# Attention and two MLPs on one core: whole-chunk weight conversion, a shorter prologue, and other steps for the second MLP's weights

## Chip, core and metric

The kernel runs on one core of a Trainium2 chip. The metric is the device time of one execution in microseconds (us), as the median of three runs.

## What is computed

Sliding-window attention (four plain heads, four dilated) gives 2304 tokens of 512 features; two MLPs with 2048 hidden features follow. The weights come as float64, q, k and v as float32.

```python
scores = scale * np.matmul(q, k.transpose(0, 1, 3, 2))      # masked to a window
attn = softmax(scores); x = matmul(attn, v)                 # (2304, 512)
h = x @ w_in;  r = np.maximum(h, 0.0)
x = (s * (r * r) + b) @ w_out                               # first MLP
h = x @ w_in2; g = h * np.cos(h)
out = g @ w_out2                                            # second MLP
```

## The kernel before

Tokens are cut into five tiles (`SIZES` = 384, 384, 512, 512, 512), the hidden features into 16 chunks. A **step** `p` is one chunk of one tile of one MLP: steps 0 to 79 are the first MLP (tile = p // 16), 80 to 159 the second. In each step TensorE (PE) makes the hidden block h (`mm_in`), and two steps later adds the chunk to the four output blocks y (`mm_out`); ScalarE (ACT) and VectorE (DVE) make g from h in between (`relu2`). Tile 0 of the first MLP multiplies in full float32; all others split each operand into a high and a low part and use three passes.

Attention for tile 0 (8 units) runs ahead of all, as a **prologue** of steps k in the loop over `range(n0 + 4)`: scores and softmax of unit k, `a_norm` of k-1, `a_transpose` of k-3, `a_pv` of k-4. The other 40 units run in pairs, inside the MLP steps that `DUO` lists: scores (PE) and softmax (DVE, then ACT's exp) in step p, `a_norm` (DVE) and `a_transpose` (PE tp, then an ACT copy to pt) in p+1, `a_pv` (PE pv, reads pt) in p+2.

A float64 weight half-chunk (128x512; even k is w_in, odd k is w_out) is **converted** to float32: `w_load` (an SP DMA of 512 KB into a stage buffer, five of them), `w_float` (two ACT instructions, L117 and L118) and `w_join` (four DVE instructions, L124 to L133). For the first MLP `w_whole(n)` brings the joins up to half-chunk n, with one float ahead; `w_split` makes high and low parts in tiles 0 and 1. The second MLP's half-chunks are converted in the first MLP's tiles 1 to 4 (`BG` = 4, 8, 10 and 10 of them, evenly spread by a formula), cut into parts by `w_cut` one step later, written to DRAM, and fetched back by `w_fetch`.

Each engine runs its instructions in the order in which the program issues them; within a step that is `mm_in`, events of phase 0, the last `mm_out` of a tile, `w_point`, `relu2`, other `mm_out`s, events of phases 1 and 2.

Of the kernel before, what the change touches and what calls it, by code (L numbers as in the profile page):

```python
# [31 lines left out]
W_FIRST, W_STEPS = (7, 8, 9, 10), {8: 1, 9: 2, 11: 3}  # L32
# [4 lines left out]
WPRE, W_PACE = 4, 2.0  # L37
IN_CUT = 13

BG = (0, 4, 8, 10, 10)  # L40
PB, PK = 64, 96
# [13 lines left out]
def attention_then_two_mlps(ctx, tc, qk_p, qk_d, v_p, v_d, mask_p, mask_d, w1, w2, sv, bv, out):  # L55
# [7 lines left out]
    xspool = pool("xs", 4)  # L63
# [30 lines left out]
    last_two = []  # L94
    after_att = []

    def w_load(m, k, stage):  # L100
        raw_w[m, k] = stage
        nc.sync.dma_start(stage[:, :DM], (w1, w2)[m][k])

    def w_float(m, k):
        words = raw_w[m, k][:, :DM].bitcast(U32).rearrange("p (n two) -> p n two", two=2)
        low, high = words[:, :, 0], words[:, :, 1]
        if m == 0 and k + 2 < 2 * NFC:
            a = wpool.tile([P, DM], I32, tag=f"wl{k + 2}", name=f"wa{m}_{k}")
        elif m == 0:
            if not last_two:  # L110
                last_two.append(wpool.tile([P, 2, DM], I32, tag="raw2", name="last_two"))
            a = last_two[0][:, k % 2, :]
        else:
            a = late[0].tile([P, DM], I32, tag=f"wa{k % 2}", name=f"wa{m}_{k}")
        w32[m, k] = a
# [4 lines left out]
    def w_join(m, k):  # L120
        words = raw_w[m, k][:, :DM].bitcast(U32).rearrange("p (n two) -> p n two", two=2)
        low, high = words[:, :, 0], words[:, :, 1]
        a = w32[m, k]
# [11 lines left out]
    def w_split(k):  # L135
        a = w32.pop((0, k)).bitcast(F32)
        wh[0, k] = wpool.tile([P, DM], F32R, tag=f"wh{k}", name=f"wh0_{k}")
        wl[0, k] = wpool.tile([P, DM], F32R, tag=f"wl{k}", name=f"wl0_{k}")
        nc.scalar.copy(wh[0, k], a)
        nc.vector.tensor_tensor(out=wl[0, k], in0=a, in1=wh[0, k].bitcast(F32), op=ALU.subtract)  # L140


    def w_cut(k):
        a = w32.pop((1, k))
        hi = raw_w.pop((1, k)).bitcast(F32R)[:, :DM]
        cut[k] = scratch.tile([P, 2, DM], F32, tag=f"cut{k}", name=f"cut{k}")
        nc.scalar.copy(hi, a.bitcast(F32))
        nc.vector.tensor_tensor(out=a.bitcast(F32R), in0=a.bitcast(F32), in1=hi.bitcast(F32), op=ALU.subtract)
        nc.sync.dma_start(cut[k][:, 0, :], hi.bitcast(F32))
        nc.sync.dma_start(cut[k][:, 1, :], a.bitcast(F32))  # L150

    def w_fetch(k):
        wh[1, k] = wpool.tile([P, DM], F32R, tag=f"wh{k}", name=f"wh1_{k}")
        wl[1, k] = wpool.tile([P, DM], F32R, tag=f"wl{k}", name=f"wl1_{k}")
        nc.sync.dma_start(wh[1, k].bitcast(F32), cut[k][:, 0, :])
        nc.sync.dma_start(wl[1, k].bitcast(F32), cut[k][:, 1, :])
# [72 lines left out]
    def a_softmax(i):  # L229
# [3 lines left out]
        sm = d["place"](3, [nr, nb, nk]) if "place" in d else ap_.tile([nr, nb, nk], F32, tag="sm", name=f"sm{i}")  # L233
# [31 lines left out]
    def a_transpose(i, ps, copy=None):  # L265
        d = st[i]
        nb, nq, nk = d["nb"], d["nq"], d["nk"]
        nr = 2 * nq
        acc = ps.tile([P, 512], F32, tag=ps_tag[ps.name], name=f"tp{i}")
        for j in range(nb):  # L270
            nc.tensor.transpose(acc[:nk, j * nr : (j + 1) * nr], d["sm"][:, j, :], ident[:nr, :nr])  # L271
        pt = d["place"](4, [nk, 384]) if "place" in d else ap_.tile([nk, 384], F32, tag="pt", name=f"pt{i}")
        (copy or nc.vector.tensor_copy)(pt, acc[:nk, :384])
        d["pt"] = pt
# [37 lines left out]
    def x_split(m, t, cc):  # L312
        x = xspool.tile([P, 2, T], F32R, tag="xs", name=f"xs{m}_{t}_{cc}")[:, :, : SIZES[t]]
# [5 lines left out]
    def mm_in(m, t, fc, ps):  # L319
        h = ps.tile([P, 512], F32, tag=ps_tag[ps.name], name=f"h{m}_{t}_{fc}")  # L320
        hps[m, t, fc] = h
        for cc in range(NCC):
            cs = slice(cc * P, (cc + 1) * P)
            if m == 0 and t == 0:
                w = w32[m, 2 * fc].bitcast(F32)
# [5 lines left out]
            hi, lo = wh[m, 2 * fc][:, cs], wl[m, 2 * fc][:, cs]  # L331
# [4 lines left out]
    def mm_out(m, t, fc):  # L336
# [48 lines left out]
    whole_g = []  # L385

    def relu2(t, fc):
# [43 lines left out]
    with tc.manual_schedule():  # L431
# [4 lines left out]
        def w_load_to(n):  # L436
            while wq[0] < min(n, 2 * NFC):
                w_load(0, wq[0], stage.tile([P, DM], I64, tag=f"s{wq[0] % 5}", name=f"stage{wq[0]}"))
                wq[0] += 1

        def w_whole(n):

            q = wq
            n = min(n, 2 * NFC)
            while q[2] < n:
                while q[1] < min(q[2] + 2, 2 * NFC):
                    w_load_to(q[1] + 1)
                    w_float(0, q[1])
                    q[1] += 1
                w_join(0, q[2])  # L450
                q[2] += 1
            w_load_to(q[2] + 1 + AHEAD)

# [19 lines left out]
        for k in range(n0 + 4):  # L473
# [3 lines left out]
            if 0 <= k - 1 < n0:  # L477
                a_norm(k - 1)
            if 0 <= k - 3 < n0:
                a_transpose(k - 3, ps_a)  # L480
            if 0 <= k - 4 < n0:
                a_pv(k - 4, ps_y, f"y{k % NCC}")
            if k in W_STEPS:
                w_whole(W_STEPS[k])
# [29 lines left out]
        def w_point(p, half):  # L514
            if p < NFC:
                w_whole(int(W_PACE * (p + half / 2)) + WPRE)
            if half == 0 and 0 <= p - IN_CUT < NFC:
                w_split(2 * (p - IN_CUT))
            if half == 1 and 0 <= p - NFC < NFC:
                w_split(2 * (p - NFC) + 1)  # L520


        k = 0
        for t, n in enumerate(BG):
            for i in range(n):
# [3 lines left out]
                def load(k=k):  # L529
                    n = k % 2 if k < BG[1] else (k - BG[1]) % 3  # L530
                    place, tag = (late[0], f"raw{n}") if n < 2 else (wpool, "raw2")
                    w_load(1, k, place.tile([P, DM], I64, tag=tag, name=f"raw{k}"))

                at((p - 1, ph), load)
                at((p, ph), lambda k=k: w_float(1, k))
                at((p, ph), lambda k=k: w_join(1, k))
                at((p + 1, ph), lambda k=k: w_cut(k))
                k += 1
        assert k == 2 * NFC
# [5 lines left out]
        for p in range(NP + LAG[1]):  # L545
# [135 lines left out]
```

## Time and profile before

| | |
|---|---|
| median of three runs | 926.11 us (925.14 to 926.75) |
| the profiled execution | 924.52 us, its span 922.7 us |
| PE busy | 895.6 us (97%) |
| DVE busy | 590.2 us (64%) |
| ACT busy | 507.5 us (55%) |
| mean granted TensorE clock | 0.99 |

Times in the profile count from the first instruction. A PE row's end is modelled, so rows overlap; the distance between starts tells the real rate. Idle time in brackets stands with what ended it.

### The profile page before, as it was taken

Reading aid. Unit: us, or ns where it says so; the run is one execution under the profiler, and the core shown is the slowest. Engines: PE = TensorE matmul, PEld = TensorE weight load, DVE = VectorE, ACT = ScalarE, POOL = GpSimd, SP = SyncE. Lnnn points to the kernel's source line nnn. Section 1 sums busy time; section 2 is a strip of 40 time slices with the busy share of each in tenths; the row PEclk is TensorE's granted clock in tenths of the full one; section 3 lists DMA queues with packets and bytes.
Section 4 is the critical chain, followed back from the end, with each engine's and each line's share of the span. In section 5 each row is a group of like instructions: output and inputs, shape, how many; then the busy total and the mean of one; then the engine's idle time right before and its main releaser. Section 6 shows DMA issues by size and latency. Waiting matters only on the chain.

```text
span 922.7 us, 13285 instructions
## 1 busy us (share of the span) xinstructions
PE 895.6 (97%) x4888; PEld 755.4 (82%) x4888; DVE 590.2 (64%) x1160; ACT 507.5 (55%) x1162; POOL 0.7 (0%) x6
## 2 busy tenths in 40 slices
PE   6899999989999989999999999999999999999998
PEld 5566679889888877778888899999988888888886
DVE  6888868666565665557464766665755665566554
ACT  5767757666564654546353654645544554454443
POOL 0000000000000000000000000000000000000000
PEclk9799999999999999999999999999999999999999
DMA  9767424332534433436799700000000010001001
GB/s 261 245 224 241 138 72 156 105 119 88 173 129 138 143 122 125 156 101 215 251 319 309 256 16 1 20 16 1 20 15 1 1 45 1 1 1 47 0 1 46
DMA packets 45536, 99.64 MB, mean 108 GB/s; under 512 B 5440, under 2 KB 12064, under 8 KB 45472
## 3 DMA queue, kind: packets, MB, share of 16 engines
q1 hardware_dynamic: 45472, 98.80, 32.1%
q8 instruction: 39, 0.64, 0.3%
q14 instruction: 25, 0.20, 0.1%
HBM read 75.71 MB, written 23.07 MB: 107 GB/s over the span
## 4 chain that ended last, share of the span: by engine, by line
PE 88%; DVE 7%; ACT 3%; issue 1%; DMA 0%; SPq 0%; DVEq 0%
PE h L332 13%; PE h L333 13%; PE h L334 13%; PE y L349 12%; PE y L350 12%; PE y L351 12%; PE y L346 4%; PE h L326 4%; PE sc L220 2%; PE pv L283 2%; ACT sm L250 2%; PE tp L271 1%; DVE wa L133 1%; DVE wa L130 1%; DVE nmax L247 1%
## 5 line engine op out<-in xcount | busy, mean ns | idle before, releaser
L332 PE MATMUL h<-xs,wh 128*128 128x512 f32 (+1 forms) x576 | 218.6, 379 | 0.0
L349 PE MATMUL y<-g,wh 128*128 128x512 f32 (+1 forms) x576 | 214.9, 373 | 0.0
L333 PE MATMUL h<-xs,wh 128*128 128x512 f32 (+1 forms) x576 | 214.9, 373 | 0.0
L334 PE MATMUL h<-xs,wl 128*128 128x512 f32 (+1 forms) x576 | 214.8, 373 | 0.0
L351 PE MATMUL y<-g,wl 128*128 128x512 f32 (+1 forms) x576 | 213.7, 371 | 0.0
L350 PE MATMUL y<-g,wh 128*128 128x512 f32 (+1 forms) x576 | 213.6, 371 | 0.0
L332 PEld LDWEIGHTS h<-xs,wh 128*128 128x128 f32 x576 | 109.0, 189 | 15.7
L334 PEld LDWEIGHTS h<-xs,wl 128*128 128x128 f32 x576 | 108.8, 189 | 15.3
L333 PEld LDWEIGHTS h<-xs,wh 128*128 128x128 f32 x576 | 109.0, 189 | 14.8
L351 PEld LDWEIGHTS y<-g,wl 128*128 128x128 f32 x576 | 108.1, 188 | 15.1
L349 PEld LDWEIGHTS y<-g,wh 128*128 128x128 f32 x576 | 108.2, 188 | 14.8
L350 PEld LDWEIGHTS y<-g,wh 128*128 128x128 f32 x576 | 108.1, 188 | 14.7
L416 ACT ACTIVATE n<-n 128x512 f32<-128x512 f32 (+1 forms) x80 | 47.2, 590 | 102.5 <-DVE n L410 102.3
L406 ACT ACTIVATE n<-h,pmagic 128x512 f32<-128x512 f32 (+1 forms) x80 | 51.6, 646 | 87.0 <-PE h L334 86.9
L407 DVE TENSOR_SCALAR n<-n 128x512 f32<-128x512 f32 (+1 forms) x80 | 32.0, 400 | 86.6 <-ACT n L406 86.5
L422 DVE SCALAR_TENSOR_TENSOR n<-n,h 128x512 f32<-128x512 f32 (+1 forms) x80 | 50.7, 633 | 55.2 <-ACT n L417 55.2
L390 ACT ACTIVATE r<-h 128x512 f32<-128x512 f32 (+1 forms) x80 | 44.1, 551 | 67.3 <-PE h L334 58.8
L250 ACT ACTIVATE sm<-sm,nmax 96x80 f32<-96x80 f32 (+1 forms) x140 | 49.5, 355 | 46.1 <-DVE nmax L247 46.1
L400 DVE CAST g<-r 128x512 fp32r<-128x512 f32 (+1 forms) x64 | 26.1, 408 | 69.0 <-ACT r L398 59.5
L124 DVE TENSOR_SCALAR wa<-wa 128x512 f32<-128x512 f32 x62 | 26.2, 423 | 42.4 <-ACT wa L117 39.7
L410 DVE SCALAR_TENSOR_TENSOR n<-n,r 128x512 f32<-128x512 f32 (+1 forms) x80 | 51.1, 638 | 2.8
L409 DVE SCALAR_TENSOR_TENSOR r<-n,h 128x512 f32<-128x512 f32 (+1 forms) x80 | 50.7, 634 | 2.8
(81 smaller groups left out, 1060.6 us busy)
## 6 DMA issues: line engine op xcount, KB each, us to landing
stage<-w SPq DMA_DIRECT2D x32, 512.0 KB, 4.7
raw<-w SPq DMA_DIRECT2D x32, 512.0 KB, 4.6
cut<-raw SPq DMA_DIRECT2D x32, 256.0 KB, 2.1
cut<-wa SPq DMA_DIRECT2D x32, 256.0 KB, 2.5
wh<-cut SPq DMA_DIRECT2D x32, 256.0 KB, 3.9
wl<-cut SPq DMA_DIRECT2D x32, 256.0 KB, 4.4
qk<-qk_d SPq DMA_DIRECT2D x20, 352.0 KB, 3.4
qk<-qk_p SPq DMA_DIRECT2D x20, 304.0 KB, 2.9
```

Source lines behind the costliest of these rows:

```text
L250: nc.scalar.activation(out=sm[:, j, :], in_=sm[:, j, :], func=AF.Exp, bias=nmax[:, j : j + 1], scale=1.0, accum_out=ssum[:, j : j + 1],)
L332: nc.tensor.matmul(h[:, : SIZES[t]], hi, x[:, 0, :], start=cc == 0, stop=False)
L333: nc.tensor.matmul(h[:, : SIZES[t]], hi, x[:, 1, :], start=False, stop=False)
L334: nc.tensor.matmul(h[:, : SIZES[t]], lo, x[:, 0, :], start=False, stop=cc == NCC - 1)
L349: nc.tensor.matmul(y[:, : SIZES[t]], hi, g[:, 0, :], start=fc == 0, stop=False)
L350: nc.tensor.matmul(y[:, : SIZES[t]], hi, g[:, 1, :], start=False, stop=False)
L351: nc.tensor.matmul(y[:, : SIZES[t]], lo, g[:, 0, :], start=False, stop=fc == NFC - 1)
L406: nc.scalar.activation(out=n, in_=h[:, : SIZES[t]], func=AF.Identity, scale=1.0 / TWO_PI, bias=pmagic)
L409: nc.vector.scalar_tensor_tensor(out=r, in0=n, scalar=-C1, in1=h[:, : SIZES[t]], op0=ALU.mult, op1=ALU.add)
L410: nc.vector.scalar_tensor_tensor(out=n, in0=n, scalar=-C2, in1=r, op0=ALU.mult, op1=ALU.add)
L416: nc.scalar.activation(out=r, in_=r, func=AF.Sin, scale=0.5)
L422: nc.vector.scalar_tensor_tensor(out=r, in0=r, scalar=-1.0, in1=h[:, : SIZES[t]], op0=ALU.add, op1=ALU.mult)
```

## The change

Three things change.

1. **First MLP's weights.** Conversion goes by whole chunks (128x1024, both halves in one instruction) from chunk 4 on; chunks 0 to 3 go by halves, in the order of `W_ORDER` (chunk, first half, halves). `W_PACE` says how far the joins go in which step. Stage buffers are four whole chunks (two of them in the pool that later holds xs), chosen by chunk % 4. The split into parts is by whole chunks, in steps 14 to 29.
2. **Prologue.** One step shorter: transposes of k-2, pv of k-3; joins come after all its attention work.
3. **Second MLP's weights.** `BG_STEPS` lists the steps of each tile, none of which starts a pair of units; the cut comes at the start of the next step. The fetch is by whole chunks, both parts at once.

```diff
-W_FIRST, W_STEPS = (7, 8, 9, 10), {8: 1, 9: 2, 11: 3}
+W_FIRST, W_STEPS = (7, 8, 9, 10), {9: 1, 10: 3}
 DUO = ((), (3, 6, 9, 12), (0, 2, 5, 7, 10, 12), (0, 2, 5, 7, 10, 12), (1, 4, 8, 11))
-WPRE, W_PACE = 4, 2.0
-IN_CUT = 13
+W_ORDER = [(0, 0, 1), (1, 0, 1), (2, 0, 1), (0, 1, 1), (3, 0, 1), (1, 1, 1), (4, 0, 2), (2, 1, 1), (5, 0, 2), (3, 1, 1)]
+W_ORDER += [(f, 0, 2) for f in range(6, NFC)]
+W_PACE = [5, 6, 8, 9, 11] + [p + 7 for p in range(5, NFC)]
+CUT = 14
 BG = (0, 4, 8, 10, 10)
+BG_STEPS = ((), (3, 6, 9, 14), (1, 3, 4, 6, 8, 9, 13, 15), (0, 2, 3, 5, 6, 7, 9, 10, 13, 15), (0, 2, 3, 5, 6, 8, 10, 11, 13, 14))
...
+    def w1_load(fc, h, n):
+        if fc not in raw_w:
+            place, tag = ((stage, f"s{fc % 4}") if fc % 4 < 2 else (xspool, f"xs{fc % 2}"))
+            raw_w[fc] = place.tile([P, 2, DM], I64, tag=tag, name=f"stage{fc}")
+        for k in range(h, h + n):
+            nc.sync.dma_start(raw_w[fc][:, k, :], w1[2 * fc + k])
...
-        def w_whole(n):
+        def w_whole(n, more=1):
             q = wq
-            n = min(n, 2 * NFC)
-            while q[2] < n:
-                while q[1] < min(q[2] + 2, 2 * NFC):
+            n = min(n, len(W_ORDER))
+            while q[2] < n or q[1] < min(n + more, len(W_ORDER)):
+                while q[1] < min(q[2] + 1 + more, n + more, len(W_ORDER)):
                     w_load_to(q[1] + 1)
-                    w_float(0, q[1])
+                    w1_float(*W_ORDER[q[1]])
                     q[1] += 1
-                w_join(0, q[2])
-                q[2] += 1
-            w_load_to(q[2] + 1 + AHEAD)
+                if q[2] < n:
+                    w1_join(*W_ORDER[q[2]])
+                    q[2] += 1
+            w_load_to(q[2] + 1 + (AHEAD if q[2] < 10 else 2))
...
-        for k in range(n0 + 4):
+        for k in range(n0 + 3):
...
-            if 0 <= k - 3 < n0:
-                a_transpose(k - 3, ps_a)
-            if 0 <= k - 4 < n0:
-                a_pv(k - 4, ps_y, f"y{k % NCC}")
+            if 0 <= k - 2 < n0:
+                a_transpose(k - 2, ps_a)
+            if 0 <= k - 3 < n0:
+                a_pv(k - 3, ps_y, f"y{k % NCC}")
...
-                b = t * NFC + (2 if t == 1 else 0) + (i + 0.5) * (NFC - (2 if t == 1 else 0)) / n
-                p, ph = int(b), 1 + int(b % 1 >= 0.5)
...
+        for k, p in enumerate(t * NFC + step for t, steps in enumerate(BG_STEPS) for step in steps):
+            at((p - 1, 1), lambda k=k: w2_load(k))
+            at((p, 1), lambda k=k: w2_float(k))
+            at((p, 1), lambda k=k: w2_join(k))
+            at((p + 1, 0), lambda k=k: w2_cut(k))
```

**Order on ACT, step 4 of tile 0** (wa and stage: the weights of the half-chunk or chunk named; r and g: relu and its square; sm8, sm9: exp of the first pair; pt: copy of its transposes). Before:

```order
L250 ACTIVATE sm9_611,ssum9_615<-sm9_611,nmax9_613 128x96 x3
L117 ACTIVATE wa0_12_632<-stage12_559 128x512
L118 ACTIVATE stage12_559<-stage12_559 128x512
L390 ACTIVATE r0_4_641<-h0_0_4_619 128x384
L396 ACTIVATE g1_513<-r0_4_641 128x384
L117 ACTIVATE wa0_13_648<-stage13_585 128x512
L118 ACTIVATE stage13_585<-stage13_585 128x512
L273 COPY pt8_661<-tp8_657 96x384
L273 COPY pt9_667<-tp9_663 96x384
```

The same place in the change:

```order
L277 ACTIVATE sm9_566,ssum9_570<-sm9_566,nmax9_568 128x96 x3
L109 ACTIVATE wa6_587<-stage6_508 128x1024
L110 ACTIVATE stage6_508<-stage6_508 128x1024
L109 ACTIVATE wa7_594<-stage7_511 128x1024
L110 ACTIVATE stage7_511<-stage7_511 128x1024
L421 ACTIVATE r0_4_604<-h0_0_4_574 128x384
L425 ACTIVATE g1_109<-r0_4_604 128x384
L300 COPY pt8_615<-tp8_611 96x384
L300 COPY pt9_621<-tp9_617 96x384
```

Two whole chunks, 6 and 7, now stand between the exps and the copies of the first pair's transposes.

**Order on the SP queue, loads of tile 0** in the change (x2: both halves of a chunk):

```order
L135 DMA stage4_446<-w1 128x512 x2
L135 DMA stage2_160<-w1 128x512
L135 DMA stage5_468<-w1 128x512 x2
L135 DMA stage3_417<-w1 128x512
L135 DMA stage6_508<-w1 128x512 x2
L135 DMA stage7_511<-w1 128x512 x2
L231 DMA qk10_538<-qk_p 128x608
```

stage4 takes stage0's place and stage7 takes stage3's, so each load now waits for the last join that reads the chunk four before; in the old order a load waited for the half-chunk five before.

**Order on DVE, step 7 of tile 1** (sm22, sm23: a pair that starts there). Before:

```order
L247 TENSOR_REDUCE nmax23_1771<-sm23_1769 96x4
L124 TENSOR_SCALAR wa1_1_1778<-wa1_1_1778 128x512
L127 TENSOR_SCALAR wa1_1_1778<-wa1_1_1778 128x512
L130 SCALAR_TENSOR_TENSOR wa1_1_1778<-raw1_1693,wa1_1_1778 128x512
L133 ISA wa1_1_1778<-raw1_1693,wa1_1_1778 128x1024
L261 TENSOR_SCALAR ssum22_1764<-ssum22_1764 96x4
```

The same pair in the change:

```order
L123 ISA wa2_1_1534<-raw1_1489,wa2_1_1534 128x1024
L175 TENSOR_TENSOR wa2_1_1534<-wa2_1_1534,raw1_1489 128x512
L150 TENSOR_TENSOR wl0_9_1585<-wa9_683,wh0_9_1584 128x1024
L429 CAST g0_1_7_1591<-r1_7_1588 128x384
L430 TENSOR_TENSOR g0_1_7_1591<-r1_7_1588,g0_1_7_1591 128x384
L265 SCALAR_TENSOR_TENSOR sm22_1606<-sc22_1566,m_d_98 96x320
L274 TENSOR_REDUCE nmax22_1608<-sm22_1606 96x4
```

The join stood between the pair's maxima and its sums; now it and its cut stand ahead of the pair's first instruction.

## Rows read from the trace of the kernel before

**Rows 1.** The page: busy time of each engine, share of the span, instructions

```profile
PE 895.6 (97%) x4888; PEld 755.4 (82%) x4888; DVE 590.2 (64%) x1160; ACT 507.5 (55%) x1162; POOL 0.7 (0%) x6
```

**Rows 2.** Waits of PE over the span: total us, times, longest

```profile
PE tp L271 <- DVE ssum L261: 8.2, 4, 2.8
...
PE tp L271 <- DVE sm L263: 2.0, 7, 0.4
```

**Rows 3.** PE's timeline from 172.2 us: start, us, instruction, idle before

```profile
172.19 0.33 PE L350 MATMUL y<-g,wh 128*128 128x384 f32 x1
172.37 0.34 PE L351 MATMUL y<-g,wl 128*128 128x384 f32 x1
174.47 0.50 PE L271 MATMUL tp<-ident,sm 96*80 96x96 f32 x4 [1.77 <-DVE ssum L261]
```

**Rows 4.** Stretches, PE alone: stretch, PE busy (x), PEclk, DMA share, GB/s

```profile
194.80:198.10 3.30, 3.30 (x13) 0.50 0.24 88
...
345.00:348.30 3.30, 3.13 (x11) 0.50 0.10 37
```

**Rows 5.** DVE's timeline, tile 1, step 7

```profile
168.03 0.48 DVE L247 TENSOR_REDUCE nmax<-sm 96x4 f32<-96x320 f32 x1
171.08 0.43 DVE L124 TENSOR_SCALAR wa<-wa 128x512 f32<-128x512 f32 x1 [2.57 <-ACT wa L117]
...
173.44 0.16 DVE L261 TENSOR_SCALAR ssum<-ssum 96x4 f32<-96x4 f32 x1
```

**Rows 6.** ACT's timeline there, the instruction behind the last exp

```profile
170.41 0.64 ACT L117 ACTIVATE wa<-raw 128x512 f32<-128x512 f32 x1
```

**Rows 7.** DVE's timeline, tile 3, step 1

```profile
343.01 0.69 DVE L148 TENSOR_TENSOR wa<-wa,raw 128x512 fp32r<-128x512 f32 x1 [1.98 <-ACT raw L147]
```

**Rows 8.** DVE's timeline, end of the prologue and first steps of tile 0

```profile
22.92 0.55 DVE L273 COPY first<-tp 80x384 f32<-80x384 f32 x1
...
31.92 0.42 DVE L124 TENSOR_SCALAR wa<-wa 128x512 f32<-128x512 f32 x1
...
34.28 0.42 DVE L124 TENSOR_SCALAR wa<-wa 128x512 f32<-128x512 f32 x1
...
51.18 0.45 DVE L238 SCALAR_TENSOR_TENSOR sm<-sc,m_p 128x288 f32<-128x288 f32 x1
...
55.23 0.42 DVE L124 TENSOR_SCALAR wa<-wa 128x512 f32<-128x512 f32 x1
```

**Rows 9.** PE's timeline, tile 0: chunks 0 to 2, then 5 and 6

```profile
30.78 9.72 PE L326 MATMUL h<-xy,wa 128*128 128x384 f32 x24
...
55.80 2.75 PE L326 MATMUL h<-xy,wa 128*128 128x384 f32 x8
...
61.91 2.85 PE L326 MATMUL h<-xy,wa 128*128 128x384 f32 x8
```

**Rows 10.** Groups of DVE by form: busy us, mean ns, idle before

```profile
L401 DVE TENSOR_TENSOR g<-r,g 128x512 fp32r<-128x512 f32 x48 | 33.2, 693 | 1.6
...
L400 DVE CAST g<-r 128x512 fp32r<-128x512 f32 x48 | 20.4, 425 | 53.8 <-ACT r L398 44.2 <-PE sc L220 9.5
...
L401 DVE TENSOR_TENSOR g<-r,g 128x384 fp32r<-128x384 f32 x16 | 8.9, 559 | 0.6
L400 DVE CAST g<-r 128x384 fp32r<-128x384 f32 x16 | 5.7, 359 | 15.2 <-ACT r L398 15.2
```

**Rows 11.** DMA issues, 34 to 46 us: size, median us to landing

```profile
stage<-w SPq DMA_DIRECT2D x5, 512.0 KB, 3.3
```

**Rows 12.** DMA issues, 411 to 413 us (two loads 0.5 us apart)

```profile
raw<-w SPq DMA_DIRECT2D x2, 512.0 KB, 4.7
```

**Rows 13.** The loads of L102 between 30 and 70 us

```profile
DMA to landing us min/median/max: 3.1/4.3/6.8
```

**Rows 14.** ACT's timeline from 415 us

```profile
416.23 0.66 ACT L117 ACTIVATE wa<-raw 128x512 f32<-128x512 f32 x1 [4.25 <-DMA raw<-w]
...
417.35 0.83 ACT L273 COPY pt<-tp 80x384 f32<-80x384 f32 x2
```

More of the change, by code (lines that the diff above doesn't have):

```diff
@@ L93, in attention_then_two_mlps, with words, w_float, w_join @@
     raw_w, w32 = {}, {}
-    last_two = []
     after_att = []
[L100 to L115, printed above, removed]
+    def words(raw):
+        w = raw.bitcast(U32).rearrange("p (n two) -> p n two", two=2)
+        return w[:, :, 0], w[:, :, 1]
+    def w_float(raw, a):
+        low, high = words(raw)
         nc.scalar.activation(out=a.bitcast(F32), in_=high.bitcast(F32), func=AF.Abs)
         nc.scalar.activation(out=low.bitcast(I32), in_=low, func=AF.Copy, scale=2.0**-29)
[L120 to L123, printed above, removed]
+    def w_join(raw, a):
+        low, high = words(raw)
         nc.vector.tensor_scalar(
@@ L133, in w_join @@
         nc.vector.tensor_tensor(out=a, in0=a, in1=low.bitcast(I32), op=ALU.add)
[L135 to L146, printed above, removed]
+    flat = lambda tile, h, n: tile[:, h : h + n, :].rearrange("p h n -> p (h n)")
@@ new lines, in w2_load, with w2_float, w2_join, w2_cut @@
+    def w2_load(k):
+        n = k % 2 if k < BG[1] else (k - BG[1]) % 3
+        place, tag = (late[0], f"raw{n}") if n < 2 else (wpool, "raw2")
+        raw_w["2", k] = place.tile([P, DM], I64, tag=tag, name=f"raw{k}")
+        nc.sync.dma_start(raw_w["2", k], w2[k])
+    def w2_float(k):
+        w32["2", k] = late[0].tile([P, DM], I32, tag=f"wa{k % 2}", name=f"wa2_{k}")
+        w_float(raw_w["2", k], w32["2", k])
+    def w2_join(k):
+        w_join(raw_w["2", k], w32["2", k])
+    def w2_cut(k):
+        a = w32.pop(("2", k))
+        hi = raw_w.pop(("2", k)).bitcast(F32R)[:, :DM]
+        fc = k // 2
+        if fc not in cut:
+            cut[fc] = scratch.tile([P, 2, 2, DM], F32, tag=f"cut{fc}", name=f"cut{fc}")
@@ L159, in attention_then_two_mlps, with w2_fetch @@
+        nc.sync.dma_start(cut[fc][:, 1, k % 2, :], a.bitcast(F32))
+    def w2_fetch(fc):
+        for w, n, l in ((wh, 0, "wh"), (wl, 1, "wl")):
+            w[1, fc] = wpool.tile([P, 2, DM], F32R, tag=f"{l}{fc}", name=f"{l}1_{fc}")
+            nc.sync.dma_start(w[1, fc].bitcast(F32), cut[fc][:, n])
     eppool = pool("ep", 1)
@@ L232, in a_softmax @@
         nr = 2 * nq
[L233 removed]
+        sm = d["sm"] if "sm" in d else ap_.tile([nr, nb, nk], F32, tag="sm", name=f"sm{i}")
         if dil:
@@ L514, in w_point @@
         def w_point(p, half):
[L515 to L525, printed above, removed]
-                b = t * NFC + (2 if t == 1 else 0) + (i + 0.5) * (NFC - (2 if t == 1 else 0)) / n
-                p, ph = int(b), 1 + int(b % 1 >= 0.5)
[L529 to L539, printed above, removed]
+            if p < NFC and half == 0:
+                w_whole(W_PACE[p])
+            if half == 0 and 0 <= p - CUT < NFC:
+                w1_split(p - CUT)
+        for k, p in enumerate(t * NFC + step for t, steps in enumerate(BG_STEPS) for step in steps):
[3 more added lines that the diff above has]
+            at((p + 1, 0), lambda k=k: w2_cut(k))
+        assert [len(steps) for steps in BG_STEPS] == list(BG)
         def fire(p, phase):
```

73 lines of the change are left out of this document (41 added, 32 removed).

## The prediction

> **What bounds the kernel.** I read the page first: PE is busy for 895.6 of 922.7 us [rows 1], so a change can only pay where PE stands still or runs slowly. Busy time hides slow running, so next come the waits of PE and its clock. Outside the prologue PE waits almost only for the transposes (tp) of attention pairs. The first transpose of a pair waited 8.2 us in four places, the second 2.0 us in seven [rows 2]; one of the seven, 0.37 us at 55 us, lies in tile 0, so tiles 1 to 3 lose 8.2 + 1.6 = 9.8 us in ten waits. The true loss is somewhat more: a matmul row is 0.34 us long, but starts lie 0.17 us apart, so a wait begins some 0.16 us before its row counts it [rows 3]; ten times 0.16 is 1.6 us. And the granted clock fell to 0.50, the lower level (1.2 GHz), behind the two longest of these waits, for 3.3 us each in which PE did half the work: 2 x 1.5 = 3 us, and as a part of it was idle anyway, 2.9 [rows 4]. Together 9.8 + 1.6 + 2.9 = 14.3 us is what tiles 1 to 3 lose. From 500 us on no tp runs, and I find nothing to gain there.
>
> Why the transposes wait is seen on DVE. In step 7 of tile 1 the maxima of the pair end at 168.5 us, but the next thing in DVE's order is a join. That waits for its float, which on ACT stands behind the pair's exps, and so starts at 171.08; the sums come at 173.44 [rows 5, 6]. The exps had ended at 170.4 [rows 6]. Without the join the first sum could have started before 170 and both normalisations been done by about 171.2, while PE came to the transpose at 174.47 - 1.77 - 0.16 = 172.5 [rows 3]. In tile 3, step 1, it is not the join but a cut, whose DVE half waited 1.98 us for ACT [rows 7].
>
> **Part 3, the second MLP's steps.** In the changed order a join or cut never stands between a pair's maxima and its sums; it has moved ahead of the pair. So nine of the ten waits should go. What is late next: the join, its cut (0.7 us) and a whole split (1.2 us, below) now come before the pair's scores are read. For step 7 of tile 1, laying these instructions one behind the other on DVE and ACT, I estimate that the pair's maxima come 1.5 us later than in rows 5, the exps end at 170.4 + 1.5 = 171.9 and the second normalisation at 172.85 (two small instructions and one of 0.5 us). PE needs it 0.33 us (the first transpose) after 172.5. So the cover in tile 1 is nothing to spare, but enough; in tiles 2 and 3 a step is over 1 us longer and I find 1.5 us or more. In tile 3, step 1, the last y of tile 2 makes the pair late whatever the conversions do: the exps end 0.6 us (ACT's half of the cut) before 343.0, at 342.4 [rows 7], the second normalisation comes at 343.4, and of that wait 1.0 us stays, while the clock should hold. Gain: 14.3 - 1.0 = 13.3 us. Bounds: 9.8 us if only the waits as the rows count them go and the clock gives nothing; 16 if that pair loses nothing either and the clock returns a little more.
>
> **Part 2, the prologue.** Each attention step on DVE is 2.2 us and now holds a copy of transposes one step earlier, so the last steps come 0.47 us (one copy) later: copy of unit 6 at 22.92 + 0.47 = 23.4 [rows 8], of unit 7 at 24.0 (its transposes take 0.5 us from 23.5). The first join follows at 24.5 and ends at 26.95, pv 7 is done by 25.5, and h of chunk 0 starts at about 27.0 instead of 30.78 [rows 9]. That is 3.8 us earlier on PE, but PE then runs into DVE.
>
> **Part 1, the chain that sets tile 0.** A half join is 34.28 - 31.92 = 2.36 us [rows 8]. A 1024-wide one is in no row. It is at least 2.36 and at most 4.71 us. From 384 to 512 columns the tensor-tensor form grows by 134 ns and the copy form by 66 ns [rows 10]; four times that for 512 more columns is 0.54 and 0.26 us, for two instructions of each form, so 2.36 + 1.6 = 3.96 us. I take that. A 1024-wide ACT instruction, likewise between 0.64 [rows 6] and 1.28, is taken as 1.1, near the upper end.
>
> The new thing is a load that waits for the chunk four before. Joins 0 to 3 start at 24.5 + 2.36 each; join 3, the w_out half of chunk 0, ends at 34.0. Only then can SP issue the two halves of chunk 4. One load alone lands in 3.3 us [rows 11], two together in 4.7 [rows 12]; I take 4.7 (ends: 3.3, and 5.6 with other traffic), so 38.8. Joins 4 and 5 are done at 38.7. The float needs 1.1 us, join 6 starts at 40.0 (1.3 us lost on DVE), then 40.0 + 3.96 + 2.36 + 3.96 = 50.3 for the pair's softmax, against 51.18 [rows 8]. From there to chunk 5's h it is 55.80 - 51.18 = 4.62 us [rows 8, 9]: 54.9. Of the 3.8 us only 0.9 are left. That wait on DVE costs PE 2 to 3 us before the transposes, which the next wait swallows.
>
> The next one is on ACT, in step 4. Chunk 7's load waits for the last half of chunk 3, whose join comes 4.05 us after the softmax began (55.23 - 51.18) [rows 8]: 50.3 + 4.05 + 2.45 = 56.8. It lands at 61.5. ACT's order there is float 6, float 7, relu 4, and then the two copies of the pair's transposes; float 6 is over by 55.5, float 7 holds ACT to 61.5 and takes 2.1 us, relu and square 1.0, the copies 1.8: 65.4. PE has done h 5 and y 3 by 60.1 (two times 2.6 us) and stands at pv until the copies come. pv ends at 65.9, and h of chunk 6 starts at 66.0 instead of 61.91 [rows 9]: 4.1 us late. A stall of 5 us is longer than the ones behind which the clock fell, 2.8 us at most [rows 2, 4], so I add 1.5 us for one more stretch at half clock. Tile 0: 5.6 us lost. After it DVE is ahead (4 us a chunk against 5.2 for PE) and the loads too, so nothing is won back and nothing more lost; tile 0 is then PE's. Bounds: with both loads at 3.3 us the two waits shrink by 1.4 us each, which leaves 1.3 with no clock stretch; with 5.6 each and two stretches at half clock it is 4.1 + 1.8 + 3.0 = 9 us.
>
> That ACT does nothing else while it waits for a load is in the trace: at 416.23 it had waited 4.25 us for one, and only behind that float came two pt copies [rows 14]. The Trainium skill says as much (Perfetto Trace Analysis, Tensor Engine Instruction: ACT, DVE and GpSimd take their instructions strictly in order, PE may reorder weight loads). By that rule the term of tile 0 stands at 5.6 us; were the copies able to pass the waiting float, it would be a gain of 0.9, and the forecast 6.5 us lower. The rows fit the rule.
>
> **No cost, and why.** The merged split instructions save some 0.15 us each on DVE and ACT, which are not the bound in tile 1. The xs tiles of two column blocks come free 0.7 us later, behind which stands a whole mm_out of 2.1 us or more; the fetches have 14 steps of lead. If this cover fails, each tile boundary costs under 1 us.
>
> **Sum.** 5.6 - 13.3 = -7.7 us. Made against the profiled execution, 924.5, this is 916.8. That execution is 1.6 us under the median of the runs shown, so for a median I give 918.4, rounded to 918. About 0.2%, 1.8 us, is what a measurement of this kernel can tell from no change.
>
> **Rivals.**
> - *The loads land quickly and ACT's hold is short.* For: the queue is nearly empty then, and one load alone lands in 3.3 us [rows 11]. Against: two halves are issued together [rows 12]. Tile 0 loses 1.3: 926.1 - 13.3 + 1.3 = 914. Chance 0.22.
> - *The moved conversions make the next pair late.* DVE in tile 1 has nothing to spare by the walk above; were each pair behind a conversion 0.5 to 1 us late, with the clock falling as before, half of the 13.3 us would stay: 926.1 - 6.6 + 5.6 = 925. For: the walk's margin of zero. Against: its terms are the longest seen. Chance 0.09.
> - *Slower: ACT's hold comes back at each pair of tile 0.* With four whole-chunk places, one load late makes the next join late, and so the next load. It decides where a load takes longer than the two joins between (2 x 3.96 = 7.9 us). The longest load in tile 0 took 6.8 us, the middle one 4.3 [rows 13]. Three more holds of 5.6 us would give 918.4 + 16.8 = 935. Chance 0.05.
> - *The steps of the second MLP don't matter*, if something other than join and cut held the sums: 926 + 5.6 = 932. Rows 5 leave little room for it. Chance 0.02.
>
> **Numbers.** The forecast has what is left, 0.62. Its own bounds, with 9.8 to 16 us gained and 1.3 to 9 lost, run from 911.4 to 925.3; the first rival lies inside. I give 911.5 to 924, which leaves out the two slow rivals, half of the second and the corners. Faster by over 0.2% (under 924.3): 0.62 + 0.22 + a third of the second rival, less 0.01 for a forecast at its worst end, is 0.86; same 0.07; slower 0.07.
>
> **What would show it.** In the profile after: h of chunk 0 at about 27 us; an ACT float of chunk 7 that waits some 5 us for a stage load before 62 us, two pt copies behind it, and PE idle before pv until 65; the granted clock at 0.50 right after; then no wait of tp over 0.5 us in tiles 1 to 3 but the one near 343, and no stretch at half clock there. PE's waits for tp in those tiles should fall from 9.8 to about 1 us. It is wrong if pv in step 5 does not wait, if tp in tile 1 still waits for DVE's sums, or if the waits go and the time does not.

## The result, and the profile after

| | before | after |
|---|---|---|
| median us of six runs (range) | 925.1 (923.6 to 926.8) | 929.7 (929.3 to 931.6) |
| ratio, 95% interval | | 1.0054, 1.0039 to 1.0069 |
| profiled execution, its span | 924.5, 922.7 | 930.6, 928.8 |

The change is slower by half a per cent; the forecast was 918, range 911.5 to 924. (It was made against 926.1, the median of the first three runs of before; all six have 925.1.) The time lies in four places, read off PE's timeline as the start of the first h of each stretch (us of the span; in brackets the time since the line above):

| | before | after |
|---|---|---|
| h of chunk 0, tile 0 | 30.78 | 30.96 |
| first h of tile 1 | 123.12 (92.3) | 133.17 (102.2) |
| first h of tile 2 | 217.88 (94.8) | 220.72 (87.6) |
| first h of the second MLP | 518.59 (300.7) | 520.14 (299.4) |
| first h of its tile 2 | 651.06 (132.5) | 657.10 (137.0) |
| end of the last matmul | 918.83 (267.8) | 924.86 (267.8) |

In these executions nothing was won in the prologue, 10 us were lost in tile 0, tiles 1 to 3 won what was forecast, and from 500 to 530 us something new was lost. The page's first line of after, which answers to [rows 1]:

```profile
PE 903.5 (97%) x4888; PEld 762.1 (82%) x4888; DVE 587.3 (63%) x1096; ACT 504.4 (54%) x1122; POOL 0.7 (0%) x6
```

The waits of PE over the span of after (total us, times, longest), which answer to [rows 2]:

```profile
PE h L361 <- ACT xs L345: 5.2, 1, 5.2
PE pv L310 <- ACT pt L300: 5.0, 1, 5.0
...
PE h L362 <- DVE xs L346: 1.8, 1, 1.8
...
PE tp L298 <- DVE sm L290: 1.1, 3, 0.6
```

The 8.2 us of tp on DVE's sums are gone. In their place stand two single waits of 5 us, one in tile 0 (pv) and one where the second MLP begins (xs, the high and low parts of a tile's input, which ACT and DVE split). During each of them a stretch at the lower clock level (1.2 GHz) begins; the stretches of [rows 4] are gone. PE of after in windows (stretch, PE busy, PEclk, DMA share, GB/s):

```profile
66.41:73.24 6.83, 3.97 (x28) 0.50 1.02 411
...
516.97:527.21 10.24, 5.26 (x15) 0.50 0.67 218
```

**Tile 0** went as the forecast walks it, only later throughout. PE's timeline of after (start, us, instruction, idle before), which answers to [rows 9]:

```profile
30.96 10.32 PE L355 MATMUL h<-xy,wa 128*128 128x384 f32 x24 [1.21 <-DVE wa L123]
...
58.89 2.75 PE L355 MATMUL h<-xy,wa 128*128 128x384 f32 x8
...
69.27 1.55 PE L310 MATMUL pv<-pt,v 96*64 96x64 f32 x24 [5.05 <-ACT pt L300]
70.75 1.65 PE L355 MATMUL h<-xy,wa 128*128 128x384 f32 x2
```

ACT's timeline of after, chunks 6 and 7 and the copies of the first pair:

```profile
57.40 1.11 ACT L109 ACTIVATE wa<-stage 128x1024 f32<-128x1024 f32 x1
...
65.78 1.12 ACT L109 ACTIVATE wa<-stage 128x1024 f32<-128x1024 f32 x1 [6.21 <-DMA stage<-w]
...
68.76 0.83 ACT L300 COPY pt<-tp 96x384 f32<-96x384 f32 x2
```

DVE's timeline of after, the join of chunk 4, the next one, and the pair's softmax, which answers to [rows 8]:

```profile
43.86 0.69 DVE L114 TENSOR_SCALAR wa<-wa 128x1024 f32<-128x1024 f32 x1 [1.21 <-ACT wa L109]
...
47.84 0.42 DVE L114 TENSOR_SCALAR wa<-wa 128x512 f32<-128x512 f32 x1
...
54.26 0.45 DVE L265 SCALAR_TENSOR_TENSOR sm<-sc,m_p 128x288 f32<-128x288 f32 x1
```

Chunk 4's join waited 1.21 us for its float, and the pair came late; chunk 7's float stood 6.21 us on its load, the pt copies came behind it, and pv waited. The load came late for want of a buffer: SP's queue stood 9.5 us, until 60.7 us, for a join (L123 is a join's last instruction), the one of chunk 3's last half. SP's waits of after from 50 to 66 us:

```profile
SPq L135 <- DVE wa L123: 15.3, 2, 9.5
```

**The boundary.** Five of the eight conversions' floats from step 3 of tile 4 on wait for their raw load, longer each time. ACT's timeline of after, four of the five, the last float and the split of xs:

```profile
451.47 0.66 ACT L109 ACTIVATE wa<-raw 128x512 f32<-128x512 f32 x1 [3.55 <-DMA raw<-w]
...
464.49 0.67 ACT L109 ACTIVATE wa<-raw 128x512 f32<-128x512 f32 x1 [5.69 <-DMA raw<-w]
...
495.07 0.67 ACT L109 ACTIVATE wa<-raw 128x512 f32<-128x512 f32 x1 [7.00 <-DMA raw<-w]
...
513.63 0.66 ACT L109 ACTIVATE wa<-raw 128x512 f32<-128x512 f32 x1 [7.09 <-DMA raw<-w]
...
518.48 0.65 ACT L109 ACTIVATE wa<-raw 128x512 f32<-128x512 f32 x1
...
519.59 1.73 ACT L345 CAST xs<-back 128x384 fp32r<-128x384 f32 x4
```

PE's timeline of after, the first h of chunk 13 of tile 4 and the first h of the second MLP:

```profile
498.14 0.39 PE L361 MATMUL h<-xs,wh 128*128 128x512 f32 x1
...
520.14 0.69 PE L361 MATMUL h<-xs,wh 128*128 128x384 f32 x1 [5.18 <-ACT xs L345]
```

SP's timeline of after shows why; the load for step 13 is the L159 row, and h of chunk 13 began at 498.14:

```profile
504.25 0.32 SPq L176 DMA_DIRECT2D cut<-raw  x1
504.98 0.32 SPq L177 DMA_DIRECT2D cut<-wa  x1
505.39 0.39 SPq L182 DMA_DIRECT2D wh<-cut  x1
505.83 0.64 SPq L182 DMA_DIRECT2D wl<-cut  x1
506.53 0.45 SPq L159 DMA_DIRECT2D raw<-w  x1
```

The load stands behind the step's store of cut, which waits for ACT's cut of the chunk before, and behind the fetch, which waits for PE. SP's waits of after from 443 to 448 us show the fetch (L182):

```profile
SPq L182 <- PE y L380: 5.6, 1, 5.6
```

From 456 to 520 us they show the store (L176), and the fetch waits 2.7 us in all:

```profile
SPq L176 <- ACT raw L174: 21.7, 6, 3.8
SPq L176 <- DMA raw<-w: 16.2, 4, 4.7
```

By these rows the fetch makes the first load late and the store carries the delay on: a float that is late makes its cut late, the cut the store, the store the next load, and that load the next float. Against the first h of the step for which they load, the loads of steps 3, 5, 8, 10 and 13 were issued 1.2, 3.2, 4.8, 6.1 and 8.4 us late. At step 15 the split of xs stands behind it all. The two waits for xs, 5.2 + 1.8, and half of the 5.26 us that PE was busy at half clock come to 9.6 us.

### The profile page after: what moved, and what is told of

It is laid out like the page before. It is cut to its first block, busy times and chain, and to the rows that moved or that the text cites. A ratio compares the mean times of both kernels' runs of the same rounds, so it can differ in the third digit from the quotient of the medians.

```text
span 928.8 us, 13071 instructions
## 1 busy us (share of the span) xinstructions
PE 903.5 (97%) x4888; PEld 762.1 (82%) x4888; DVE 587.3 (63%) x1096; ACT 504.4 (54%) x1122; POOL 0.7 (0%) x6
## 4 chain that ended last, share of the span: by engine, by line
PE 88%; DVE 4%; DMA 3%; ACT 3%; issue 1%; SPq 0%; DVEq 0%; ACTq 0%
PE h L361 13%; PE h L362 12%; PE h L363 12%; PE y L378 12%; PE y L379 12%; PE y L380 12%; PE h L355 4%; PE sc L247 3%; PE y L375 3%; PE pv L310 3%; PE tp L298 2%; DMA raw<-w 2%; DMA stage<-w 1%; DVE wa L123 1%; DVE wa L120 1%
## 5 line engine op out<-in xcount | busy, mean ns | idle before, releaser
L362 PEld LDWEIGHTS h<-xs,wh 128*128 128x128 f32 x576 | 108.8, 189 | 16.9 <-DVE xs L346 2.2
L458 DVE TENSOR_TENSOR g<-n,g 128x512 fp32r<-128x512 f32 (+1 forms) x80 | 50.4, 631 | 0.7 <-ACT g L457 0.7
```

Of the source, the lines that this page charges most:

```text
L362: nc.tensor.matmul(h[:, : SIZES[t]], hi, x[:, 1, :], start=False, stop=False)
L458: nc.vector.tensor_tensor(out=g[:, 1, :], in0=r, in1=g[:, 0, :].bitcast(F32), op=ALU.subtract)
```

## The experiments

The ratio is to runs of the kernel before on the same chip.

| run | edit | us | ratio, 95% interval |
|---|---|---|---|
| a1_steps_only | before, new steps | 921.8 | 0.9951, 0.9931 to 0.9970 |
| a2_load_first | after, load ahead of fetch | 920.0 | 0.9941, 0.9921 to 0.9960 |
| a3_last_late | after, last step 15 for 14 | 927.9 | 1.0024, 1.0008 to 1.0040 |
| a4_float_late | after, float of chunk 7 a step later | 930.4 | 1.0053, 1.0035 to 1.0071 |
| b1_halves_load_first | a1, load ahead of fetch | 912.0 | 0.9852, 0.9839 to 0.9866 |
| b2_short_prologue | b1, short prologue | 913.0 | 0.9858, 0.9843 to 0.9873 |
| b3_long_prologue | a2, long prologue | 918.2 | 0.9919, 0.9906 to 0.9931 |
| b4_five_buffers | a2, five staging buffers | 911.5 | 0.9847, 0.9830 to 0.9863 |
| c1_best | b4, long prologue | 909.6 | 0.9834, 0.9815 to 0.9852 |
| c2_again | after, once more | 929.9 | (one run) |
| d1_buffers_only | after, five staging buffers | 921.6 | 0.9961, 0.9948 to 0.9975 |
| d2_before_load_first | before, load ahead of fetch | 924.8 | 1.0002, 0.9991 to 1.0013 |

### The boundary: a2, a3, a1, d2, b1

a2, in the loop over the steps:

```diff
             f = p - NFC * (NTILE - 1) - LAG[0]
+            fire(p, 1)
             if 0 <= f < NFC:
                 w2_fetch(f)
-            fire(p, 1)
             fire(p, 2)
```

> The changed kernel with one edit: in tile 4 the raw load of a step is issued ahead of the step's fetch of wh and wl instead of behind it. Theory A (the raw load stands on SP behind fetches that wait for PE's last use of wh and wl, so ACT's float waits about 7 us and xs behind it comes 5 us late): the floats of tile 4 wait under 2 us for the load, the wait for xs at the boundary falls from 5.2 us to under 1, the 10 us at clock 0.50 behind it go, 919 to 921 us against 929.7. Theory B (the place of the last two conversions ahead of xs is the cause, whenever their loads land): at most 2 us of it goes, 927 to 929 us.

920.0, 9.7 us under the changed kernel. SP's timeline of a2 has the load ahead of the fetch, 1.1 us before h of chunk 13 (500.50) instead of 8.4 after it:

```profile
499.41 0.51 SPq L159 DMA_DIRECT2D raw<-w  x1
500.47 0.32 SPq L182 DMA_DIRECT2D wh<-cut  x1
```

ACT's timeline of a2, the floats of steps 13 and 14:

```profile
505.38 0.67 ACT L109 ACTIVATE wa<-raw 128x512 f32<-128x512 f32 x1 [0.70 <-DMA raw<-w]
...
510.25 0.66 ACT L109 ACTIVATE wa<-raw 128x512 f32<-128x512 f32 x1
```

No wait for xs is left, and PE ran at the upper level from 76.9 us on. Theory A, as far as the load's place goes. The store of cut still stands ahead of the load, and still waits for ACT (17.6 us between 456 and 520 us), but with the fetch out of the way that cost PE nothing.

a3, in the last row of BG_STEPS:

```diff
-(0, 2, 3, 5, 6, 8, 10, 11, 13, 14)
+(0, 2, 3, 5, 6, 8, 10, 11, 13, 15)
```

> The changed kernel with the last conversion at step 15 of tile 4 instead of 14, so that it stands behind the split of xs on ACT and DVE; the one at step 13 stays. Theory A: the float at step 13 still waits some 7 us for its load and relu and xs are still late, only the 1.1 us of float and 2.3 us of join ahead of xs go: 926.5 to 928.5 us, and PE still waits 2 to 4 us for xs. Theory B: the wait for xs falls under 1 us and the stretch at clock 0.50 goes: 919 to 921 us.

927.9; PE waited 3.4 us for xs, and 6.8 us passed at half clock there. Theory A again: the float of step 13 alone keeps most of the loss.

a1, in the kernel before (the loop over BG with its half steps goes):

```diff
+        for k, p in enumerate(t * NFC + step for t, steps in enumerate(BG_STEPS) for step in steps):
...
+            at((p - 1, 1), load)
+            at((p, 1), lambda k=k: w_float(1, k))
+            at((p, 1), lambda k=k: w_join(1, k))
+            at((p + 1, 0), lambda k=k: w_cut(k))
```

> The kernel before with nothing but the new table of steps for the second MLP's conversions (load one step ahead, float and join in one step, cut at the next step's start); prologue, tile 0 and the fetch by halves stay. Theory A (the moved conversions are what won, and the loss at the first to second MLP boundary comes from the raw loads queued behind the merged 512 KB fetches): the 9 to 10 us of waits of tp in tiles 1 to 3 go, the two stretches at clock 0.50 go, and little is lost at the boundary: 911 to 914 us, ratio 0.985 to 0.988. Theory B (the boundary loss comes from the steps 13 and 14 themselves, whose conversions stand ahead of xs on ACT and DVE): the same gain of 13 to 14 less a boundary loss of 8 to 10: 919 to 922 us, with PE waiting about 5 us for xs near 500 us of the span.

921.8: the number that theory B gave. The waits of PE in a1:

```profile
PE h L333 <- ACT xs L317: 5.6, 1, 5.6
...
PE h L334 <- DVE xs L318: 1.8, 1, 1.8
...
PE tp L272 <- DVE sm L264: 1.4, 4, 0.6
```

So the fetch by halves of before gives 5.6 and 1.8 us, much as after: my word "merged" in theory A falls. Theory B gave the number, but not the cause: in b1, below, steps 13 and 14 stay and the loss goes. What costs is the new steps together with a load that is queued one step ahead, behind a fetch of any size.

d2 puts the load (with all other events of phases 1 and 2) ahead of the fetch in the kernel before, with its old steps:

> The kernel before, old steps, old fetch, with nothing but the raw load of tile 4's steps issued ahead of the fetches. Theory A (the place on the queue cost nothing in the old steps, since there no float stood ahead of xs without its load: it needs the new steps 13 and 14): 924 to 926 us, same as before. Rival (the load's place was always worth something): 915 to 921 us.

924.8, ratio 1.0002 (0.9991 to 1.0013): with the old steps the place on the queue costs nothing. Which trait of the new steps makes it cost (where they lie, or that the cut comes at the start of the next step), no run parts. b1 has both, a1's steps and the load ahead:

> The kernel before with the new table of steps (as in a1) and, in tile 4, the raw load of a step issued ahead of the step's fetches; prologue, tile 0 and the fetch by halves of before. Theory A (a raw load behind fetches that wait for PE, whether merged or by halves, is what made a1 lose 5.8 + 2.3 us of waits for xs and 10 us at clock 0.50): that loss goes as in a2, 911 to 913.5 us, ratio 0.985 to 0.9875, no wait of PE over 1 us between 480 and 530 us. Theory D (only the merged fetch leaves enough room, by halves there are twice as many DMAs that hold the queue): 916 to 921 us with a wait for xs of 3 us or more.

912.0, no wait of PE between 480 and 530 us, and no stretch at half clock from 34 us to the last matmul: theory A, and D falls. From the first h of tile 1 to the first of the second MLP b1 needs 382.2 us where before needs 395.5: 13.3 us.

### Tile 0: a4, b4, d1

a4, the float of chunk 7 in step 5:

```diff
-                w_whole(W_PACE[p])
+                w_whole(W_PACE[p], 0 if p == 4 else 1)
```

> The changed kernel with the float of chunk 7 in step 5 of tile 0 instead of step 4, so that ACT copies pt of the first pair before it waits for that chunk's load; joins stay where they are. Theory A (the hold of ACT by this float is what cost tile 0 the late pv and h6 and the half clock behind them): the gap of about 5 us ahead of pv near 69 us goes to under 1, and the stretch at clock 0.50 from 66 to 73 us shrinks: 923 to 925.5 us against 929.7. Theory C (the join of 4 us on DVE or the load of chunk 7 itself is the limit, and the wait only moves to relu of step 5 and to y): 928 to 930 us, with PE waiting as long for g or wa one or two steps later.

930.4, no gain, as theory C said. pv no longer waits, but two floats now stand in a row at step 5, each on its load, and relu behind them; PE then waits for relu. ACT's timeline of a4:

```profile
64.94 1.17 ACT L109 ACTIVATE wa<-stage 128x1024 f32<-128x1024 f32 x1 [4.37 <-DMA stage<-w]
...
70.91 1.12 ACT L109 ACTIVATE wa<-stage 128x1024 f32<-128x1024 f32 x1 [3.75 <-DMA stage<-w]
...
72.95 0.47 ACT L421 ACTIVATE r<-h 128x384 f32<-128x384 f32 x1
```

PE's waits in a4:

```profile
PE sc L247 <- ACT r L421: 4.6, 1, 4.6
```

Whichever instruction stands behind the load pays; the load itself has to come earlier. b4 gives it a buffer:

```diff
+            if fc % 5 == 2:
+                raw_w[fc] = [stage.tile([P, DM], I64, tag="s2", name=f"stage{fc}"), wpool.tile([P, DM], I64, tag="raw2", name=f"half{fc}")]
+            else:
+                place, tag = ((stage, f"s{fc % 5}") if fc % 5 < 2 else (xspool, f"xs{fc % 5 - 3}"))
...
```

> The changed kernel with the load ahead of the fetch (a2) and five staging buffers of whole chunks instead of four (the fifth in two halves: 4 KB more of staging and the tile raw2, whose own use comes later; its chunks 7 and 12 are converted as two halves). No chunk's load then waits for the last half of an early chunk. Theory A (loads that wait for a buffer, with ACT held behind them, are tile 0's loss): no wait of ACT for a load over 1.5 us after h0, the pv wait of 5 us and the clock at 0.50 near 66 to 73 us go, 910 to 914 us against 920.0. Theory C (the wide instructions are: a join of 4 us on DVE and floats of 1.1 us on ACT in front of softmax and relu): 917 to 920 us, with PE's waits in tile 0 now put down to DVE.

911.5, 8.5 us under a2: theory A. ACT's waits for loads in tile 0 of after (32 to 133 us; total us, times, longest):

```profile
ACT wa L109 <- DMA stage<-w: 14.9, 4, 6.2
```

The same of b4 (32 to 125 us):

```profile
ACT wa L109 <- DMA stage<-w: 4.4, 2, 2.5
```

I had put the bound at 1.5 us a wait, and 2.5 was seen, but no wait of pv is left, nor a stretch at half clock behind it. (b4 also converts chunk 7 in two halves, and no run parts that from the buffer; but its halves hold ACT for 2.3 us, from 58.1 to 60.4, against 2.0 for the whole chunk in after, and wait for no load.) Tile 0 takes 94.3 us against 92.3 of before; these 2 us I did not follow further. With the buffers alone:

> The changed kernel with the five staging buffers of b4 alone; the load stays behind the fetch. Theory A (two separate losses, each with its own cause): tile 0's 10 us go, the boundary keeps its wait of 5 us for xs and some 7 to 10 us at clock 0.50: 919 to 922.5 us, and what the two mends give apart (9.7 and this) adds up to what b4 has with both. Rival (the boundary's loss was set off by tile 0's late loads, through a later SP queue): the boundary loss falls below 3 us, 911 to 914 us.

921.6, with the 4.8 us for xs and 10.2 us of half clock still at the boundary. The mends take 9.7 (a2) and 8.1 (d1) from 929.7; both together (b4) take 18.2. In ratios to before on the same chip that is 1.1, 0.9 and 2.1%. Two separate losses.

### The prologue: b3, b2, c2, and all mends: c1

b3 and c1 put the long order back, with a step more in the loop; b2 does the reverse in b1, and moves the third join from step 11 to 10:

```diff
-            if 0 <= k - 2 < n0:
-                a_transpose(k - 2, ps_a)
             if 0 <= k - 3 < n0:
-                a_pv(k - 3, ps_y, f"y{k % NCC}")
+                a_transpose(k - 3, ps_a)
+            if 0 <= k - 4 < n0:
+                a_pv(k - 4, ps_y, f"y{k % NCC}")
```

b3, the long order put back into a2, 918.2 us:

> The changed kernel with the load ahead of the fetch (a2) and the prologue as long as before (tp at step k-3, pv at k-4), whole chunks kept. Theory P: h0 at 30.5 to 31.5 us as in before, tile 0 loses its 10 us all the same, 920.5 to 923 us against 920.0 of a2. Theory R (the shorter prologue is what unsettles tile 0, by bringing h0 forward of the joins): tile 0 loses 6 us or less, 915 to 918 us.

b2, the short order put into b1, 913.0 us:

> As b1, with the prologue one step shorter (tp at step k-2, pv at k-3, third join at step 10), conversions by halves as before. Theory P (the order is shorter by up to 3 us, and it is the phase of PE's clock in the first 36 us that gives or takes it): h0 between 28 and 31 us of the span by the clock of the run, 909.5 to 913 us, the spread over the runs wider than b1's. Theory Q (in the new order PE's low clock and the steps of 2.98 us always eat the gain): h0 at 31 us or later, same as b1 within 1 us.

c2, the changed kernel again, 929.9 us:

> The changed kernel once more, for a second look at PE's clock in the prologue. Theory P (the clock's phase differs from run to run in the short order, which leaves PE at half clock in most): h0 at 31 us with the clock low till about 35.7, as in after, a2, b2 and b4, or, less often, a rise near 13 to 17 us and h0 at 28 to 29.5, as in a3 and a4. Loss at tile 0 of 10 to 12 us and at the boundary of about 10 us either way, 927 to 931 us.

c1, a2 with five buffers and the long order, 909.6 us:

> The three mends together: load ahead of the fetch (a2), five staging buffers (b4), the prologue as long as before (b3), with whole chunks and the new steps kept. Theory P (with whole chunks and halves first it is the long order that brings h0 to 28 us, since PE's clock rises near 11 us in it, and the short order keeps PE at half clock till 35 us): h0 at 28 to 28.6 us against 31.03 of b4, tile 0 as in b4, 908 to 910.5 us. Theory S (the three microseconds of h0 are taken back in tile 0, where DVE's joins set the first pair's softmax): h0 at 28 but tile 0 of 96 to 97 us in place of 94.3, 911 to 912 us, as b4.

What the profiles show of it:

| prologue, conversions | first rise of the granted clock in the record -> h of chunk 0 (us) |
|---|---|
| long, halves | before 10.4 -> 30.78; d2 9.8 -> 30.59; b1 13.5 -> 30.63; a1 13.8 -> 31.15 |
| long, whole chunks | b3 10.9 -> 28.13; c1 34.2 -> 30.18 |
| short, whole chunks | a3 12.8 -> 27.98; c2 14.7 -> 28.16; a4 16.9 -> 29.19; d1 16.9 -> 29.25; b4 35.6 -> 31.03; after 35.7 -> 30.96; a2 35.9 -> 31.24 |
| short, halves | b2 35.7 -> 32.22 |

One and the same prologue (after, c2, a3) reached h at 31 or at 28 us, by when the clock rose. The early rise does not last: in each of the nine profiles that have it, the granted clock fell to 0.50 again at 23 to 25 us and rose at 31 to 34. The profile prints a granted clock of 1.00 ahead of the first rise in its record, but the matmuls say otherwise. Groups of PE from 12.9 to 23 us in after (busy us, mean ns):

```profile
L247 PE MATMUL sc<-first_qk 128*96 128x80 f32 x32 | 6.3, 378 | 0.0
```

The same group in a3, where the clock had risen:

```profile
L247 PE MATMUL sc<-first_qk 128*96 128x80 f32 x32 | 3.6, 256 | 0.0
```

The attention steps on DVE wait for sc in after and are 2.99 us apart. DVE's timeline of after:

```profile
20.27 0.49 DVE L265 SCALAR_TENSOR_TENSOR first_qk<-sc,m_d 96x320 f32<-96x320 f32 x1 [0.70 <-PE sc L247]
...
23.26 0.49 DVE L265 SCALAR_TENSOR_TENSOR first_qk<-sc,m_d 96x320 f32<-96x320 f32 x1 [0.70 <-PE sc L247]
```

DVE's timeline of a3, where they are 2.19 us apart and wait for nothing:

```profile
18.21 0.48 DVE L265 SCALAR_TENSOR_TENSOR first_qk<-sc,m_d 96x320 f32<-96x320 f32 x1
...
20.40 0.48 DVE L265 SCALAR_TENSOR_TENSOR first_qk<-sc,m_d 96x320 f32<-96x320 f32 x1
```

Where the clock rose in time, the kernels with whole chunks reached h at 28.0 to 29.3 us in either order, and those with halves, in the long one, at 30.6 to 31.2. The 2.5 us between are not the width, for chunks 0 to 3 go by halves in both; they are the place of the joins. In before two joins stand ahead of the last copy of transposes, which the last pv waits for. DVE's timeline of before, the second of them and that copy:

```profile
26.35 0.41 DVE L124 TENSOR_SCALAR wa<-wa 128x512 f32<-128x512 f32 x1
...
29.11 0.55 DVE L273 COPY first<-tp 80x384 f32<-80x384 f32 x1
```

In b3, with the same long order, only one does. DVE's timeline of b3:

```profile
24.10 0.41 DVE L114 TENSOR_SCALAR wa<-wa 128x512 f32<-128x512 f32 x1
...
26.45 0.55 DVE L300 COPY first_v<-tp 80x384 f32<-80x384 f32 x1
```

In both, h of chunk 0 starts 1.7 us after that copy starts. From the shorter order itself no gain can be seen. In medians the long order is ahead in all three pairs (a2 to b3 1.8 us, b4 to c1 1.9, b2 to b1 1.0); in ratios to before on the same chip that is 0.22, 0.13 and 0.06%, and the intervals overlap, so none is told apart. b3 fits neither theory: h came at 28.13 where P said 30.5 or later, and tile 0 took 102.9 us, so R falls too. b2's profile, with h at 32.22, and its median, 1.0 us over b1's, are what Q said; but its runs spread over 3.4 us against 1.4 of b1, as P said. c2 shows the early rise at 14.7 that P named as the rarer case, with the same losses of 11.5 us in tile 0 and 10.7 at the boundary. c1's tile 0 took 94.0 us, against S; its h came at 30.18, with the clock low till 34.2, against P, whose range its time of 909.6 meets all the same. The clock rose early in five of six long orders and in four of eight short ones; whether the order decides that stays open.

Each row of the table is one execution, and not always the usual one. The mean granted clock of every run is on record: in b2 the profiled run has 1.000 and took 914.7 us, the other three 0.994, as has b1 with its stretch at half clock from 23.8 to 34.0 us, and they took 911.3 to 913.0. In c1 the profiled run has 0.999, the other four 0.993 to 0.996; in after it has 0.991, and four of the other five 0.985 to 0.987. Since only a record with an early rise has shown a stretch at half clock ahead of tile 0 or in its first microseconds, these runs probably rose early. So the late h of b2 and c1 speaks of one run each, and Q's "always" is not shown.

c1 beats both kernels, ratio 0.9834 (0.9815 to 0.9852). From b1, which keeps the halves, it is not told apart by the intervals: of the three changes, the steps of the second MLP, with the load ahead of the fetch, carry all of the gain that is clear of the noise.

## Why the prediction was wrong

**The step that failed is the one under "No cost": "the fetches have 14 steps of lead", and "each tile boundary costs under 1 us" if that fails.** It asked who waits for the fetch, not what waits behind it on SP. Behind it stood the raw loads, whose floats hold ACT and, at step 15, the split of xs. The boundary cost 9.7 us (a2); it was not the merged fetch that the step spoke of (a1 loses as much by halves), but the new steps of tile 4, for which no term was put down. "From 500 us on no tp runs, and I find nothing to gain there" was true and ended the walk too early: the table of steps has a row for tile 4, with steps 13 and 14 right ahead of that split, and I walked its rows for tiles 1 to 3 alone. This is also the bulk of the distance from 918: without it the time is 920.0, inside the range. That it lies inside is owed in part to the range's width, for the prologue's 4 us, below, were wrong as well.

In the profiled executions the sum went from a forecast of -7.7 us to +6.1 (930.6 against 924.5): 10.2 at the boundary (5.7 in tile 4, 4.5 in the first tile of the second MLP), 4.0 from the prologue and 0.5 from the clock in tile 0, less 0.9 more that tile 1 won.

**Part 3** was right. Forecast 13.3 us with 1.0 left in tile 3, step 1; b1 won 13.3, a2 14.2 (395.5 to 381.3), the 0.9 more in tile 1, where it has whole chunks. Of the tp waits 0.8 us are left in tiles 1 to 3, and no half clock there. The prediction's own sign against itself, that the waits go and the time does not, is what came.

**Part 2** was wrong in its base: "Each attention step on DVE is 2.2 us" holds only while PE runs at the upper level. In after it did not, PE set the step, and h came at 30.96, not 27.0. With the clock up (a3) the walk was 1 us short: join 0 at 25.40 against 24.5, h at 27.98. And most of what it forecast to win comes from the place of the joins, not from the shorter order: b3 has h at 28.13 in the long one.

**Part 1** was right in mechanism and sizes: the wide join took 47.84 - 43.86 = 3.98 us (3.96 forecast), the wide ACT instruction 1.11 (1.1). Softmax of the pair came at 54.26 (50.3), h of chunk 5 at 58.89 (54.9), chunk 7's float at 65.78 (61.5), h of chunk 6 at 70.75 (66.0): 4 to 4.8 us late each, which is the prologue's 3.96. The stretch at half clock had PE busy for 3.97 us, so by half of that it cost 2.0, not 1.5 (the same reckoning gives 3.2 for the 2.9 us of [rows 4]). 5.6 + 4.0 + 0.5 = 10.1, and the first h of tile 1 came 10.05 us late. One term does not add up: 61.5 + 2.1 + 1.0 and copies of 1.8 would be 66.4; the 65.4 that stands there needs copies of 0.8, which is what [rows 14] and the profile after (0.83 for two) show. By the Trainium skill (Perfetto Trace Analysis, Tensor Engine Instruction) ACT takes its instructions in order; the trace agrees, with the copies at 68.76 behind the float.

**Rivals.** Quick loads: no, ACT stood 6.21 us. A late next pair: no, its waits are gone. The hold at each pair of tile 0: no, after chunk 7 the next float waited 1.03 us and then PE was the bound. Steps that don't matter: no, tiles 1 to 3 won. The slower side was named, but by another mechanism.

## What to carry to other kernels

When DMAs are moved or merged, walk the issuing queue as an engine: list what stands behind each DMA that waits, and who waits for that. A load that is issued one step ahead, behind a store that waits for the previous conversion and a fetch that waits for PE, closes a loop that gets later at each turn; issue loads that wait for nothing ahead of those (here ahead of the fetch was enough). A fixed ring of buffers with a late release holds not only its load but the engine whose in-order instruction needs it; moving that instruction moves the wait (a4), another buffer takes most of it away (b4, 14.9 to 4.4 us).

## What was not expected of the hardware

The prologue of one kernel ended at 28 or at 31 us by when PE's clock rose, and the granted clock in the profile says nothing ahead of its first entry; the duration of a matmul (378 or 256 ns) does. The Trainium skill (DMA: Bandwidth & Descriptors, Issuing engines are not separate DMA queues) says that issuing from several engines saves only the sequencer's time to initiate a DMA, usually small. Here an initiation on SP takes 0.32 to 1.03 us between 500 and 520 us, but the sequencer's waits put a load 8.4 us late, and its place on that one queue was worth 9.7 us. No run here issues these DMAs from a second engine.
